# Attention inputs of three batches: 32x32 block transposes on VectorE in place of TensorE transposes

## The chip, the cores and the metric

The kernel runs on one core of one Trainium2 chip. The metric is the device time of one execution in microseconds (us). Before the change three runs took 700.96, 701.54 and 702.19 us, a median of 701.54 us.

The engines are named as in the profile: PE is TensorE's matrix multiply and PEld its weight load, DVE is VectorE, ACT is ScalarE, POOL is GpSimd, SP is SyncE, which issues nearly all loads. Each engine works through its own instructions in order. Where an instruction needs something from another engine or from a transfer, it waits for a semaphore, and all that stands behind it on its engine waits too.

## The reference, cut to what matters

```python
# batch, n_heads, seq_l, seq_g, head_dim = (4, 8, 512, 32, 64)
s_g = scale * np.matmul(q_g, k_all.transpose(0, 1, 3, 2))        # 32 global queries see all 544 keys
out_g = np.matmul(sm(s_g), v_all)
s_ll = scale * np.matmul(q_l, k_l.transpose(0, 1, 3, 2))         # local queries
s_ll = np.where(np.abs(pos[:, None] - pos[None, :]) <= 32, s_ll, -1e9)
s_lg = scale * np.matmul(q_l, k_g.transpose(0, 1, 3, 2))
out_l = np.matmul(sm(np.concatenate([s_lg, s_ll], axis=-1)), np.concatenate([v_g, v_l], axis=2))
x = attn.transpose(0, 2, 1, 3).reshape(2176, 512)
x = relu(x @ w_in) ** 2 @ w_out                                  # 512 -> 2048 -> 512
# then 8 routed experts (512 -> 1024 -> 512), one per token, added to x
```

All inputs and the output are float32. For the scores, queries and keys must lie with the head dimension on the partitions, so the loaded rows have to be turned.

## The kernel before, in words

Attention runs in blocks of 256 local queries: two blocks to a batch, eight in all (j = 0 to 7), each of two tiles "a" and "b" of 128 queries; the batch's 32 global queries ("g") go with them. The dense layer follows one block behind: while `ffn_block(j)` multiplies block j, the attention of block j + 1 is put between its steps. The whole order is written out by hand, as strings of words. `SEQ` holds batch 0 and the first half of batch 1 beside the dense layer's first two blocks and the splitting of its weights; then `EVEN` and `ODD` alternate for dense blocks 2 to 7; then a tail and the experts follow. The order of the words is the order of the instructions on every engine, the queue of SP included. The words that matter here:

- `Lq2`, `Lk10`, `Lk11` in SEQ and `lq`, `lk0`, `lk1` in EVEN and ODD load a query block (`load_q`, L316) or four heads of a batch's keys (`load_k`, L296) into a staging tile of 128 partitions x 1024 floats.
- `2q`, `q` turn a query block (`prep_q`, L357) into `qT`; `20` to `23`, `0` to `3` turn one pair of heads of the keys (`prep_k`, L344) into `kT`, which has place for one batch. In both, PE transposes 128x128 pieces into PSUM (L348 for keys, L365 for queries) and ACT copies them to SBUF (L350, L355, L367). `G` (`prep_globals`) turns the global keys and queries.
- `E` and `F` are steps of the dense layer. Steps come in pairs for a group f of 128 hidden features: `first(f)` is 12 matmuls (L739 to L741) into one of two PSUM places "h"; then ACT takes the ReLU (L743), the square is made on DVE (an `F` or `I` step, L780) or on ACT (`E`, `H`, L782), ACT casts the high part `gh` (L197), POOL or DVE subtracts the low part `gl` (L198), and `second` multiplies (L764 to L766). The square goes out with the step after `first(f)`; `first(f+2)` needs the PSUM place, and so that square. `second` runs one group behind in SEQ, two in EVEN and ODD.
- `V` loads windows of the values (L376, L413), `A` and `C`, `D` assemble and split weights of the dense layer, `r`, `s`, `R00` route, `1b` ends a tile of attention: PE turns it (L294), ACT and DVE split it into `xh` and `xl` (L197, L198), on which the first matmuls of the next dense block work.

The words around the change:

```
SEQ   ... 1g Lq2 C Lk10 A H0 1g I0 2q A C C F0 2G Lk11 E0 I0 20 C E0 21 22 F0 1b F1 23 C D F0 H1 C C V R00 2a ...
EVEN  q E F F r E r a ... E E V g b F b F b F g F s lk1 F g E V g lq F lk0 E
ODD   q E F lq G E 3 2 F 1 E F r E r 0 E r F a r lv0 ...
```

ODD belongs to dense blocks 3 and 5, with the attention blocks 4 and 6 that open batches 2 and 3; there `q` uses what `lq` of the EVEN before loaded. EVEN's `q` serves blocks 3, 5 and 7, whose loads (`Lq3`, and `lq` of ODD) stand most of a dense block ahead. Blocks 0 and 1 (batch 0) are loaded and turned in another way, which the change leaves as it is.

Of the kernel before, what the change touches and what calls it, by code (L numbers as in the profile page):

```python
# [54 lines left out]
def attention_ffn_routed_experts(  # L55
# [22 lines left out]
    nc = tc.nc  # L78
    B, H, SL, D = q_l.shape
    SG = q_g.shape[2]  # L80
    P = 128
# [3 lines left out]
    E, _, F = w1.shape  # L85
    NPAIR = H // 2
# [3 lines left out]
    TPB = SL // P  # L90
    NLT = B * TPB
    NT = NLT + 1
    SEG = 32
    WIN = 3 * SEG
# [7 lines left out]
    BLK = 2 * P  # L102
# [12 lines left out]
    def sb(tag, bufs, shape, name, dtype=F32):  # L115
        return spool.tile(shape, dtype, tag=tag, bufs=bufs, name=name + arm[0])

    def stage(name):
        return wpool.tile([P, 1024], F32, tag="w", name=f"st_{name}{arm[0]}")
# [3 lines left out]
    def pair(name):  # L123
        return ps.tile([P, 4, P], F32, tag="tr", bufs=2, name=name + arm[0])
# [6 lines left out]
    KEYS = (BLOCKS + (BLOCKS - 1) // 3) * SEG  # L131
# [38 lines left out]
    for b in range(B):  # L170
# [11 lines left out]
        out=tri, in_=tri, compare_op=ALU.is_gt, fill=0.0, base=0, pattern=[[1, P]], channel_multiplier=-1,  # L182
# [102 lines left out]
    kT, kin, qT, qin, qgT, vgr = {}, {}, {}, {}, {}, {}  # L285
# [6 lines left out]
    def transposes(o, src, n=P):  # L292
        for p in range(NPAIR):
            nc.tensor.transpose(o[:, p, 0:n], src[0:n, p * P:(p + 1) * P], ident[0:n, 0:n])  # L294

    def load_k(b, z):  # L296

        kin[b, z] = stage(f"k{b}_{z}").rearrange("p (j h d) -> p j h d", h=4, j=TPB)
        if b == 0:
            t = stage(f"k{b}_{z}_in").rearrange("p (h j d) -> p h j d", h=4, j=TPB)
            nc.sync.dma_start(t, k_l[b, 4 * z:4 * z + 4].rearrange("h (p j) d -> p h j d", j=TPB))
            puts[f"{b}{z}"] = lambda: nc.scalar.copy(kin[b, z], t.rearrange("p h j d -> p j h d"))
            return
        for h in range(4):
            nc.sync.dma_start(kin[b, z][:, :, h, :], k_l[b, 4 * z + h].rearrange("(p j) d -> p j d", j=TPB))

    def load_globals(b):  # L310
        t = stage(f"g{b}")
# [4 lines left out]
    def load_q(j):  # L316

        b, z = divmod(j, TPB // 2)
        qin[j] = stage(f"q{j}").rearrange("p (i h d) -> p i h d", h=H, i=2)
        if j < 2:  # L320
            t = stage(f"q{j}_in").rearrange("p (h i d) -> p h i d", h=H, i=2)
            nc.sync.dma_start(t, q_l[b, :, z * BLK:(z + 1) * BLK, :].rearrange("h (p i) d -> p h i d", i=2))
            engine = nc.vector if j == 0 else nc.gpsimd
            puts[str(j)] = lambda: engine.tensor_copy(qin[j], t.rearrange("p h i d -> p i h d"))
            return
        for i in range(2):
            rows = q_l[b, :, z * BLK:(z + 1) * BLK, :].rearrange("h (p i) d -> p i h d", i=2)
            nc.sync.dma_start(qin[j][:, i], rows[:, i])

    def prep_globals(b):  # L330
        kT[b] = sb("kT", 1, [P, NPAIR, KEYS], f"kT{b}")
# [10 lines left out]
        nc.scalar.copy(qgT[b], tr[:, :, 0:SG])  # L342

    def prep_k(b, p):  # L344
        tr = pair(f"ktr{b}_{p}")
        for j in range(TPB):
            two = kin[b, p // 2][:, j, 2 * (p % 2):2 * (p % 2) + 2, :]
            nc.tensor.transpose(tr[:, j, :], two.rearrange("p r d -> p (r d)"), ident)  # L348
        q = WIN * (KEYS // P) // TPB
        nc.scalar.copy(  # L350
            kT[b][:, p, 0:KEYS - SEG].rearrange("p (g q j) -> p j g q", j=TPB, q=P // TPB)[:, :, :, 0:WIN // TPB],
            tr[:, :, 0:q].rearrange("p j (g q) -> p j g q", q=WIN // TPB),
        )
        put = nc.vector.tensor_copy if b == 0 else nc.scalar.copy
        put(kT[b][:, p, KEYS - SEG:KEYS].rearrange("p (q j) -> p j q", j=TPB), tr[:, :, q:P])  # L355

    def prep_q(j):  # L357
        qT[j] = sb("qT", 1, [P, NPAIR, BLK], f"qT{j}")
        for z in range(2):
            tr = pair(f"qtr{j}_{z}").rearrange("p (a i) q -> p a i q", a=2)  # L360
            for a in range(2):
                for i in range(2):
                    h = 2 * (2 * z + a)
                    two = qin[j][:, i, h:h + 2, :]
                    nc.tensor.transpose(tr[:, a, i, :], two.rearrange("p r d -> p (r d)"), ident)  # L365
            for a in range(2):
                nc.scalar.copy(qT[j][:, 2 * z + a, :].rearrange("p (q i) -> p i q", i=2), tr[:, a])  # L367
# [208 lines left out]
    def attention_block(j, S_TAG="s", O_TAG="o", G_TAGS=("s", "o")):  # L576

        b, z = divmod(j, TPB // 2)
        gens = {
            "a": attention(2 * j, S_TAG, O_TAG), "b": attention(2 * j + 1, S_TAG, O_TAG),  # L580
            "g": attention_global(b, *G_TAGS),
        }

        def emit(what):
            if what in gens:
                next(gens[what])
            elif what == "G":
                prep_globals(b)
            elif what == "q":
                prep_q(j)  # L590
            elif what in "0123":
                prep_k(b, int(what))
            elif what == "lq":
                if j + 1 < NB:
                    load_q(j + 1)
            elif what in ("lv0", "lv1"):
                load_v_global(b, int(what[2]))
            elif b + 1 < B:
                load_globals(b + 1) if what == "lg" else load_k(b + 1, int(what[2]))

        return emit
# [649 lines left out]
    with tc.manual_schedule():  # L1251
# [3 lines left out]
        def do(what):  # L1255
# [12 lines left out]
            elif what == "V":  # L1268
                load_v(*divmod(viewed[0], 2))
                viewed[0] += 1  # L1270
            elif what[0] == "P":
                puts[what[1:]]()
            elif what == "L9":
                nc.sync.dma_start(w9[:, :, 0:E], w_gate.rearrange("(k p) e -> p k e", p=P))
                nc.sync.dma_start(w9[:, :, E:E + 1], w_skip.rearrange("(k p o) -> p k o", p=P, o=1))
            elif what[0] == "L":
                load = {"g": load_globals, "k": load_k, "q": load_q, "v": load_v_global}[what[1]]
                load(*map(int, what[2:]))
            elif what[0] in "FEIH":
                square_on[0] = nc.vector if what[0] in "FI" else nc.scalar  # L1280
                rest_on[0] = nc.gpsimd if what[0] in "FE" else nc.vector
                j = int(what[1])
                if j not in streams:
                    streams[j] = ffn_block(j, 1, (("x2", "x2"), ("s", "o"))[j])
                next(streams[j])
            elif what[0] == "R":
                j, z = int(what[1]), int(what[2])
                if (j, z) not in routes:
                    routes[j, z] = route(*outs[j][z], *(("x2",) if j == 0 else ()))
                next(routes[j, z])  # L1290
            else:
                j = int(what[0])
                if j not in emits:
                    emits[j] = attention_block(
                        j, *(("x2", "x2") if j == 2 else ("s", "o")), (("tr", "tr") if j == 1 else ("s", "o"))
                    )
                emits[j](what[1:])
# [15 lines left out]
        for j in range(2, NB):  # L1313
# [4 lines left out]
            for what in (ODD if j % 2 else EVEN).split():  # L1318
# [14 lines left out]
                elif what in route_gens:  # L1333
                    next(route_gens[what])
                    routed += 1
                    if j == NB - 1 and routed == 10:
# [4 lines left out]
                            out=count[:, 0:1], in0=count[:, 0:1], scalar1=2.0 * P, scalar2=None, op0=ALU.max  # L1341
# [29 lines left out]
        for what in TAIL.split():  # L1371
            if what == "T":
                next(ffn, None)
            elif what in "XY":
                j = "XY".index(what)
# [15 lines left out]
            elif what == "S":  # L1391
# [4 lines left out]
                    out=key, in0=key, scalar=float(SEG - P), in1=count[:, FEW[0]:FEW[0] + 1], op0=ALU.add, op1=ALU.max  # L1396
                )
                nc.vector.scalar_tensor_tensor(
                    out=key, in0=count[:, E - 1:E], scalar=float(-P), in1=key, op0=ALU.add, op1=ALU.max
                )  # L1400
                nc.vector.scalar_tensor_tensor(
                    out=key, in0=count[:, 0:1], scalar=float(SEG - 3 * P), in1=key, op0=ALU.add, op1=ALU.max
# [12 lines left out]
            elif what[0] in "gp":  # L1415
                e, j = map(int, what[1:])
# [141 lines left out]
        with tc.If(n_tok[E] <= SEG, label="few") as few:  # L1558
# [12 lines left out]
            n = AFTER * NPE  # L1571
# [71 lines left out]
```

## Time and profile before

| | before |
|---|---|
| runs | 700.96, 701.54, 702.19 us |
| the profiled execution's own time | 701.17 us |
| its span in the profile | 699.5 us |
| PE busy | 675.6 us (97%) in 6661 matmuls |
| DVE busy | 395.9 us (57%) |
| ACT busy | 365.9 us (52%) |
| POOL busy | 165.8 us (24%) |
| DMA queue of the hardware's dynamic transfers | 107296 packets, 70.62 MB |

A timeline row gives the start in us from the span's start, the length, the engine, the line, the operation, what is written from what, and how many are merged; in brackets stands idle time of the engine just before, and what ended it. An instruction row for SP is the issue of a transfer, not the transfer itself. Matmuls overlap: the length of one says less than the distance to the next start.

### The profile page before, as it was taken

The page shows a single profiled execution, that of the slowest core. Times are in us where ns is not written, and L with a number is a line of the kernel's source. Part 1 is how long each engine was busy: PE and PEld are TensorE (multiplying, and loading weights), DVE is VectorE, ACT ScalarE, POOL GpSimd, SP SyncE. Part 2 cuts the span into 40 slices and gives each one's busy share as a digit, 9 for nine tenths or more (in the row PEclk, how much of TensorE's full clock was granted, in tenths as well). Part 3 has the DMA queues.
Part 4 walks back from the last instruction along what each step waited for, and adds up shares of the span by engine and source line. Part 5 has one row for each costly group of instructions (what it writes and reads, how often), then busy time and mean ns, then how long its engine had stood idle before and what let it go on. Part 6 is the DMA issues. An engine that isn't in the chain of part 4 may idle for free. (4 is left out here: it accounts for less than half of the span.)

```text
span 699.5 us, 16771 instructions
## 1 busy us (share of the span) xinstructions
PE 675.6 (97%) x6661; PEld 565.1 (81%) x6661; DVE 395.9 (57%) x1078; ACT 365.9 (52%) x950; POOL 165.8 (24%) x220
## 2 busy tenths in 40 slices
PE   6689998999999999999999999999999999999996
PEld 4466667889888988888898888888887887898876
DVE  1899964872655175265426536534338733915985
ACT  5767568665535655453465445444334414614863
POOL 8000053453212212211212221122220432301311
PEclk9799999999999999999999999999999999999999
DMA  9999644065053501306440210410036688962930
GB/s 271 250 298 281 236 109 90 1 156 103 1 132 84 135 32 36 84 2 143 107 100 32 58 55 9 156 62 1 30 112 186 212 269 301 373 244 85 354 131 21
DMA packets 117695, 93.40 MB, mean 134 GB/s; under 512 B 83733, under 2 KB 90901, under 8 KB 117604
## 3 DMA queue, kind: packets, MB, share of 16 engines
q1 hardware_dynamic: 107296, 70.62, 36.2%
q10 hardware_dynamic: 8292, 15.48, 6.9%
q0 software_dynamic: 2016, 6.09, 2.5%
q8 instruction: 56, 0.92, 0.6%
q14 instruction: 35, 0.29, 0.1%
HBM read 79.91 MB, written 12.66 MB: 132 GB/s over the span
## 5 line engine op out<-in xcount | busy, mean ns | idle before, releaser
L198 POOL TENSOR_TENSOR gl<-g,gh 128x256 fp32r<-128x256 f32 x107 | 79.8, 746 | 297.5 <-ACT gh L197 125.6
L739 PE MATMUL h<-xh,w_in 128*128 128x256 f32 x464 | 134.9, 291 | 0.7 <-ACT xh L197 0.7
L740 PE MATMUL h<-xl,w_in 128*128 128x256 f32 x464 | 129.7, 279 | 0.3 <-DVE xl L198 0.3
L741 PE MATMUL h<-xh,w_in 128*128 128x256 f32 x464 | 129.8, 280 | 0.0
L764 PE MATMUL acc<-w_out,gh 128*128 128x512 f32 x232 | 97.6, 421 | 1.2 <-ACT gh L197 1.2
L766 PE MATMUL acc<-w_out,gl 128*128 128x512 f32 x232 | 91.9, 396 | 0.2
L765 PE MATMUL acc<-w_out,gh 128*128 128x512 f32 x232 | 91.6, 395 | 0.0
L739 PEld LDWEIGHTS h<-xh,w_in 128*128 128x128 f32 x464 | 87.1, 188 | 5.0 <-ACT xh L197 0.9
L740 PEld LDWEIGHTS h<-xl,w_in 128*128 128x128 f32 x464 | 87.2, 188 | 2.6 <-DVE xl L198 0.5
L743 ACT ACTIVATE g<-h 128x256 f32<-128x256 f32 x128 | 48.7, 381 | 74.2 <-PE h L741 44.5
L741 PEld LDWEIGHTS h<-xh,w_in 128*128 128x128 f32 x464 | 87.1, 188 | 0.0
L780 DVE TENSOR_TENSOR g<-h,g 128x256 f32<-128x256 f32 x53 | 22.2, 420 | 85.5 <-ACT g L743 85.4
L464 ACT ACTIVATE sm<-sm,mx 128x128 f32<-128x128 f32 x120 | 46.7, 391 | 44.0 <-DVE mx L462 43.9
L197 ACT CAST gh<-g 128x256 fp32r<-128x256 f32 x116 | 47.2, 407 | 42.8 <-DVE g L780 40.4
L766 PEld LDWEIGHTS acc<-w_out,gl 128*128 128x128 f32 x232 | 43.5, 188 | 12.0 <-POOL gl L198 1.4
L764 PEld LDWEIGHTS acc<-w_out,gh 128*128 128x128 f32 x232 | 43.6, 188 | 8.4 <-ACT gh L197 1.7
L765 PEld LDWEIGHTS acc<-w_out,gh 128*128 128x128 f32 x232 | 43.8, 189 | 5.7
L269 POOL TENSOR_TENSOR w_in<-st_raw_in,w_in 128x512 fp32r<-128x512 f32 x10 | 13.0, 1311 | 76.7 <-ACT w_in L265 76.7
L457 DVE TENSOR_TENSOR sm<-sc,masks_slots 128x512 f32<-128x512 f32 x30 | 20.6, 685 | 15.4 <-PE sc L444 14.4
L782 ACT ACTIVATE g<-g 128x256 f32<-128x256 f32 x63 | 26.3, 417 | 5.0 <-ACT g L743 4.0
L762 PE MATMUL acc<-st_raw_out,gh 128*128 128x512 f32 x48 | 23.9, 618 | 0.8 <-ACT gh L782 0.8
L473 PE MATMUL ptr<-ident,sm 128*128 128x128 f32 x120 | 20.3, 286 | 2.6 <-ACT sm L464 2.4
(638 smaller groups left out, 1463.9 us busy)
## 6 DMA issues: line engine op xcount, KB each, us to landing
st_e<-in_moe_w_dram SPq DMA_DIRECT2D x46, 512.0 KB, 6.5
st_raw_in<-in_moe_w_in_dram SPq DMA_DIRECT2D x16, 512.0 KB, 8.1
st_raw_out<-in_moe_w_out_dram SPq DMA_DIRECT2D x16, 512.0 KB, 8.3
st_e<-in_moe_w_dram ACTq DMA_DIRECT2D x12, 512.0 KB, 7.4
x2d<-x ACTq DMA_DIRECT2D x19, 256.5 KB, 3.6
vr<-in_v_l_dram SPq DMA_DIRECT2D x32, 128.0 KB, 3.3
st_gv<-in_v_l_dram SPq DMA_DIRECT2D x8, 512.0 KB
out_dram<-x ACTq DMA_DIRECT2D x16, 256.0 KB, 3.6
```

The source lines that it names most:

```text
L197: nc.scalar.copy(hi, src)
L198: (lo_engine or nc.vector).tensor_tensor(out=lo, in0=src, in1=hi.bitcast(F32), op=ALU.subtract)
L464: nc.scalar.activation(sm[:, hh, :], sm[:, hh, :], AF.Exp, bias=mx[:, hh:hh + 1], scale=SCALE, accum_out=osum[:, 2 * hh + g:2 * hh + g + 1],)
L739: nc.tensor.matmul(h, lhsT=wh, rhs=xh[:, k, :], start=(k == 0), stop=False)
L740: nc.tensor.matmul(h, lhsT=wh, rhs=xl[:, k, :], start=False, stop=False)
L741: nc.tensor.matmul(h, lhsT=wl, rhs=xh[:, k, :], start=False, stop=(k == KD - 1))
L743: nc.scalar.activation(g, h, AF.Relu)
L762: nc.tensor.matmul(acc[z], lhsT=gh[:, c], rhs=w, start=first_one, stop=last_one)
L764: nc.tensor.matmul(acc[z], lhsT=gh[:, c], rhs=wh, start=first_one, stop=False)
L765: nc.tensor.matmul(acc[z], lhsT=gh[:, c], rhs=wl, start=False, stop=False)
L766: nc.tensor.matmul(acc[z], lhsT=gl[:, c], rhs=wh, start=False, stop=last_one)
L782: nc.scalar.activation(square, g, AF.Square)
```

## The change

For batches 1 to 3 (b > 0, j >= 2) the loads split each head dimension into halves of 32: partition quadrant 2r + half holds head r of a pair and half the head dimension, with positions in blocks of 32 on the quadrant's partitions. A key load of four heads becomes 8 transfers of 64 KB where it was 4 of 128 KB; a query block becomes 16 of 32 KB where it was 2 of 256 KB; the contiguous run falls from 256 to 128 bytes. One 32x32 transpose on each block then puts the head dimension on the partitions. `prep_k` is two DVE transposes to a pair of heads (384 and 128 columns), `prep_q` two of 512 columns; the PE transposes, their PSUM tiles and the ACT copies of these batches are gone. The strings of words are the same.

```diff
+    def quadrants(o, src):
+        for r in range(2):
+            for half in range(2):
+                c = SEG * (2 * r + half)
+                for a in range(o.shape[1]):
+                    nc.sync.dma_start(o[c:c + SEG, a], src(r)[:, a, :, SEG * half:SEG * (half + 1)])
+
     def load_k(b, z):
-        kin[b, z] = stage(f"k{b}_{z}").rearrange("p (j h d) -> p j h d", h=4, j=TPB)
...
-        for h in range(4):
-            nc.sync.dma_start(kin[b, z][:, :, h, :], k_l[b, 4 * z + h].rearrange("(p j) d -> p j d", j=TPB))
+        kin[b, z] = stage(f"k{b}_{z}").rearrange("p (a n d) -> p a n d", a=2, d=SEG)
+        pairs = k_l[b, 4 * z:4 * z + 4].rearrange("(a r) (n p) d -> r p a n d", r=2, p=SEG)
+        quadrants(kin[b, z], lambda r: pairs[r])
...
-        for i in range(2):
-            rows = q_l[b, :, z * BLK:(z + 1) * BLK, :].rearrange("h (p i) d -> p i h d", i=2)
-            nc.sync.dma_start(qin[j][:, i], rows[:, i])
+        qin[j] = stage(f"q{j}").rearrange("p (a n d) -> p a n d", a=NPAIR, d=SEG)
+        pairs = src.rearrange("(a r) (n p) d -> r p a n d", r=2, p=SEG)
+        quadrants(qin[j], lambda r: pairs[r])
...
     def prep_k(b, p):
+        if b:
+            full = WIN * (KEYS // P)
+            src = kin[b, p // 2][:, p % 2].rearrange("p n d -> p (n d)")
+            threes = kT[b][:, p, 0:KEYS - SEG].rearrange("p (g c) -> p g c", c=P)[:, :, 0:WIN]
+            nc.vector.transpose(out=threes, in_=src[:, 0:full].rearrange("p (g c) -> p g c", c=WIN))
+            nc.vector.transpose(out=kT[b][:, p, KEYS - SEG:KEYS], in_=src[:, full:SL])
+            return
...
     def prep_q(j):
         qT[j] = sb("qT", 1, [P, NPAIR, BLK], f"qT{j}")
+        if j >= 2:
+            for a in range(0, NPAIR, 2):
+                nc.vector.transpose(
+                    out=qT[j][:, a:a + 2].rearrange("p a q -> p (a q)"),
+                    in_=qin[j][:, a:a + 2].rearrange("p a n d -> p (a n d)"),
+                )
+            return
```

## Rows read from the trace of the kernel before

**Rows 1.** The page's part 1: busy time by engine

```profile
PE 675.6 (97%) x6661; PEld 565.1 (81%) x6661; DVE 395.9 (57%) x1078; ACT 365.9 (52%) x950; POOL 165.8 (24%) x220
```

**Rows 2.** Stretches: us, busy of PE, PEld, DVE, ACT, POOL; PEclk, DMA share, GB/s

```profile
44.00:690.00 646.00, 640.84 (x6220) 540.21 (x6220) 366.36 (x1016) 338.98 (x878) 150.69 (x158) 1.00 0.43 126
...
98.40:105.50 7.10, 7.10 (x52) 6.04 (x51) 3.02 (x7) 4.91 (x13) 3.28 (x3) 1.00 0.59 134
```

**Rows 3.** PE's transposes by line: min/median/max ns, first and last start

```profile
L348 PE MATMUL ktr<-ident,st_k x64: 270/272/477, 9.0 to 365.0; 128*128 128x128 f32 x64
...
L365 PE MATMUL qtr<-ident,st_q x64: 270/273/474, 12.3 to 410.3; 128*128 128x128 f32 x64
```

**Rows 4.** Timeline of PE, start of dense block 5

```profile
351.41 1.03 PE L365 MATMUL qtr<-ident,st_q 128*128 128x128 f32 x8
352.21 0.36 PE L739 MATMUL h<-xh,w_in 128*128 128x256 f32 x1
...
355.82 0.39 PE L739 MATMUL h<-xh,w_in 128*128 128x256 f32 x1
...
357.34 1.04 PE L348 MATMUL ktr<-ident,st_k 128*128 128x128 f32 x8
358.13 0.48 PE L764 MATMUL acc<-w_out,gh 128*128 128x512 f32 x1
358.45 0.39 PE L765 MATMUL acc<-w_out,gh 128*128 128x512 f32 x1
358.68 0.39 PE L766 MATMUL acc<-w_out,gl 128*128 128x512 f32 x1
```

**Rows 5.** ACT's copies of turned keys and queries, by line

```profile
L350 ACT COPY kT<-ktr x16: 1017/1030/1104, 10.1 to 365.4; 128x480 f32<-128x480 f32 x16
...
L367 ACT COPY qT<-qtr x32: 384/404/430, 13.4 to 411.1; 128x256 f32<-128x256 f32 x32
```

**Rows 6.** Timeline of SP's queue: issues of transfers

```profile
92.45 1.23 SPq L328 DMA_DIRECT2D st_q<-in_q_l_dram  x2
...
110.83 0.45 SPq L413 DMA_DIRECT2D vr<-in_v_g_dram  x1
...
111.32 0.45 SPq L376 DMA_DIRECT2D vr<-in_v_l_dram  x1
...
329.75 1.30 SPq L308 DMA_DIRECT2D st_k<-in_k_l_dram  x2
...
343.35 1.08 SPq L328 DMA_DIRECT2D st_q<-in_q_l_dram  x2
```

**Rows 7.** DMA issues by kind: KB each, median us from issue to landing

```profile
st_k<-in_k_l_dram SPq DMA_DIRECT2D x24, 128.0 KB, 3.3
...
vr<-in_v_l_dram SPq DMA_DIRECT2D x32, 64.0 KB, 2.7
```

**Rows 8.** Timeline of DVE in SEQ, and one copy of 1024 columns by line

```profile
100.18 0.42 DVE L780 TENSOR_TENSOR g<-h,g 128x256 f32<-128x256 f32 x1
...
109.87 0.69 DVE L198 TENSOR_TENSOR xl<-xtr,xh 128x512 fp32r<-128x512 f32 x1 [2.43 <-ACT xh L197]
...
L324 DVE COPY st_q<-st_q_in x1: 693/693/693, 9.6 to 9.6; 128x1024 f32<-128x1024 f32 x1
```

**Rows 9.** Timeline of PE in SEQ, where batch 1 is turned

```profile
103.11 0.40 PE L764 MATMUL acc<-w_out,gh 128*128 128x512 f32 x1
...
110.61 0.38 PE L740 MATMUL h<-xl,w_in 128*128 128x256 f32 x1 [0.34 <-DVE xl L198]
...
112.02 0.60 PE L348 MATMUL ktr<-ident,st_k 128*128 128x128 f32 x4
112.37 0.48 PE L764 MATMUL acc<-w_out,gh 128*128 128x512 f32 x1
```

**Rows 10.** An idle stretch of PE early in the span, and the stretch behind it

```profile
19.90 1.25 PE L473 MATMUL ptr<-ident,sm 128*128 128x128 f32 x3 [2.39 <-ACT sm L464]
...
20.60:23.90 3.30, 3.24 (x70) 2.33 (x69) 3.23 (x7) 2.46 (x12) 0.00 (x0) 0.50 0.85 217
```

More of the change, by code (lines that the diff above doesn't have):

```diff
@@ L294, in transposes @@
             nc.tensor.transpose(o[:, p, 0:n], src[0:n, p * P:(p + 1) * P], ident[0:n, 0:n])
+    def quadrants(o, src):
[4 more added lines that the diff above has]
+                    nc.sync.dma_start(o[c:c + SEG, a], src(r)[:, a, :, SEG * half:SEG * (half + 1)])
     def load_k(b, z):
-        kin[b, z] = stage(f"k{b}_{z}").rearrange("p (j h d) -> p j h d", h=4, j=TPB)
         if b == 0:
+            kin[b, z] = stage(f"k{b}_{z}").rearrange("p (j h d) -> p j h d", h=4, j=TPB)
             t = stage(f"k{b}_{z}_in").rearrange("p (h j d) -> p h j d", h=4, j=TPB)
@@ L318, in load_q @@
         b, z = divmod(j, TPB // 2)
-        qin[j] = stage(f"q{j}").rearrange("p (i h d) -> p i h d", h=H, i=2)
+        src = q_l[b, :, z * BLK:(z + 1) * BLK, :]
         if j < 2:
+            qin[j] = stage(f"q{j}").rearrange("p (i h d) -> p i h d", h=H, i=2)
             t = stage(f"q{j}_in").rearrange("p (h i d) -> p h i d", h=H, i=2)
-            nc.sync.dma_start(t, q_l[b, :, z * BLK:(z + 1) * BLK, :].rearrange("h (p i) d -> p h i d", i=2))
+            nc.sync.dma_start(t, src.rearrange("h (p i) d -> p h i d", i=2))
             engine = nc.vector if j == 0 else nc.gpsimd
```

## The prediction, made before the change was run

> **What bounds the kernel now.** I read the busy times first: PE works 97% of the span, the others 57% or less [rows 1]. The table of stretches says where that holds: from 44 to 690 us PE is busy for 640.84 of 646.00 us at full granted clock [rows 2]. All turning of batches 1 to 3 lies in there. So what leaves PE is time won, as long as PE finds its next operands ready; and any wait that the change puts in front of PE is time lost.
>
> Two queues decide whether operands are ready. DVE now has to wait for the loads in its own order, and behind that wait stand the squares of the dense layer and, in SEQ, the low part `xl` (L198), without which PE has no work. SP issues the loads one by one. The timeline of SP's queue, read beside that of PE, is therefore the second view that matters.
>
> **What goes from PE.** 64 transposes each for keys and queries [rows 3]; a quarter is batch 0's and stays, so 48 + 48 go. Each is listed at 270 ns or more, but they overlap, so I take distances between starts. Eight for a query block: 351.41 to 352.21, 0.80 us. Eight for two pairs of heads: 357.34 to 358.13, 0.79 [rows 4]. Four: 112.02 to 112.37, 0.35 [rows 9]. The matmul behind such a group also starts its successor late, 0.32 us (358.13 to 358.45) against 0.23 (358.45 to 358.68) [rows 4], 0.09 to a group. A query block is 0.89 us, a batch of keys 0.79 + 2 x 0.35 + 3 x 0.09 = 1.76. For six query blocks and three batches that makes 10.6 us, 1.5% of the time. This is the most that can be won.
>
> Here a rule and the rows disagree. The Trainium skill, "VectorE: DVE Perf Modes", section "The three transpose paths", gives 390 ns for a 128x128 bf16 transpose on TensorE; an estimate by that page is 96 x 0.39 = 37 us removed. The rows are of float32 in a full pipeline and show 0.10 us each, and I go by them.
>
> **What ACT loses.** 24 copies of about 1.03 us, 24 of 0.40 [rows 5] and the short ones. I cost it at nothing: ACT is half idle and PE does not wait for it.
>
> **What DVE gains.** No row shows a block transpose. Operations of 512 and 256 columns take 0.69 and 0.42 us; a copy of 1024 columns takes 0.693 [rows 8]. The bounds for 512 columns are thus 0.35 (the copy's rate) and 1.38 (two passes); I take 0.69, the nearest in columns, and by the same line 0.55 for 384 and 0.28 for 128. A query block is 1.38 us, a pair of heads 0.83; together 18 us on an engine that is 57% busy. Away from the waits below, one step is covered by the group that `second` lags behind, so it costs nothing by itself.
>
> **What SP gains.** A query block grows from 2 transfers to 16, a tile of keys from 4 to 8. Transfers of 64 KB with 256 runs follow each other after 0.49 us (110.83 to 111.32); the new query transfers also have 256 runs each, of half the length. Two key transfers of 512 runs take 1.30 us, so 0.67 each with the gap; the new ones also have 512. A query block took 1.08 or 1.23 us and will take 16 x 0.49 = 7.8; a tile of keys goes from 2.7 to 5.4 us [rows 6]. The bounds for a query transfer are 0.25 (half, if the issue goes by bytes) and 0.67. Landing comes 2.7 us after issue for 64 KB and 3.3 for keys [rows 7]. The engines behind the queue have room: in a stretch with only runs of 256 bytes they moved 134 GB/s at 0.59 busy [rows 2], so a run costs at most 18 ns on an engine, and a query block of 4096 runs 4.6 us on 16 of them, less than its issue.
>
> The Trainium skill speaks against this: "DMA: Bandwidth & Descriptors", section "Rules for kernel authors", wants small transfers put together and calls those under 64 KB mostly overhead. With its fixed 2.0 us paid one after another (an estimate), a query block would take 32 us and the change would lose tens of us; the rows show issues 0.49 apart, each landing in its own 2.7, so I price by issues.
>
> **Where it falls on the path.** Three places.
>
> EVEN, blocks 3, 5, 7: the queries are loaded most of a block ahead, so DVE finds them landed. Gain 0.89 x 3 = 2.67.
>
> ODD, blocks 4 and 6, shown for 6. `lq` is issued from 343.35 [rows 6]; the sixteenth transfer goes at 343.35 + 15 x 0.49 = 350.7 and lands at 353.4. Two transposes: 354.8; the square behind them: 355.2. The third `first` needs that square's PSUM place. It started at 355.82 [rows 4], without PE's query transposes it could at 354.93, so PE loses 0.3. `lk0`, behind `lq`, lands at 351.2 + 7 x 0.67 + 3.3 = 359.2; DVE holds there, but the next square's place is wanted only later. Gain 0.89 + 1.76 - 0.3 = 2.35, twice: 4.7. Later loads on SP slip some 9 us (6.7 + 2.7 of added issue), in front of long waits of SP for window places.
>
> SEQ: three loads in a row. `Lq2` is issued from 92.45 [rows 6], lands at 92.45 + 7.35 + 2.7 = 102.5, is turned by 103.9, and the square that ran at 100.18 [rows 8] follows some 5 us late. PE stands from about 102 to 107.7, where `second` began at 103.11 [rows 9]. The 16 key transfers follow from 100.3; the last goes at 110.3 and lands at 113.6. Behind it on DVE stand pair 2 (0.83), a square (0.42) and `xl` (0.69): 115.6. PE's first matmul on `xl` stood at 110.61 [rows 9], having waited for it already. From there to `second` at 112.37 it was 1.76, now 1.32 without four transposes: 116.9. So SEQ as a whole loses 4.5 us, its own savings counted.
>
> PE's clock may add to that: early in the span an idle stretch of 2.39 us was followed by one at granted clock 0.50, the lower level of 1.2 GHz, for all of 3.3 us [rows 10]. Here the first idle stretch would be followed by work that waits for `xl` anyway: 4.6 us of it between 107.7 and 115.6, which even with 3.3 us at half speed is done. I count 0, with 2 as the upper end.
>
> **Sum.** 4.5 - 4.7 - 2.67 = -2.9 us on the profiled execution's 701.17, 698.3; its span is 1.7 shorter than that. The median of the runs stands 0.37 higher, so I forecast 698.7. With clock and issue prices near the rows the forecast's own range is 696 to 702.
>
> **Rivals.**
>
> *The loads stay hidden.* If query transfers issue at 0.25 us, `lq` lands at 349.8 and SEQ's keys about 4 us earlier; with landings as short as the queue's room allows, little is left of the waits. Then the whole 10.6 goes: 690.9. For it: the engines' room, and no wait of PE for these loads now. Against it: no issue on SP's queue in the rows is that short.
>
> *SP's queue puts the loads behind their use, and it is slower than before.* At 0.67 us for a query transfer, `lq` lands at 343.35 + 10.05 + 2.7 = 356.1, its square ends at 357.9, PE stands 3.0 us: ODD loses 0.35, twice. SEQ's last key lands at 116.5, `second` begins at 119.8 instead of 112.37: 7.4. Sum 0.7 + 7.4 - 2.67 = +5.4, 706.9; if the two idle stretches in ODD bring the low clock for 3.3 us each, another 3.3: 710. It decides from about 0.55 us an issue, as each 0.1 costs 1.6 in SEQ and 1.5 in each ODD. For it: transfers with 512 runs take 0.67, and the source now has one more step. Against: the run count is the same as in the 0.49 rows.
>
> *Transposes at twice the price* (1.38 for 512 columns): each ODD loses 1.38 more, SEQ 0.83: +3.6, 702.3. For it: nothing but that no row shows one.
>
> **Chances.** A difference under 0.2%, 1.4 us, can't be told from no change. Forecast 0.48 (0.36 of it faster, 0.12 the same), hidden 0.12 (faster), slow queue 0.27 (slower), dear transposes 0.13 (0.08 the same, 0.05 slower). That is 0.48 faster, 0.20 the same, 0.32 slower. The range goes from 692.5, just above the hidden case, to 707, which takes in the slow queue without clock loss.
>
> **What would show it.** Right: SP issues of queries 0.49 apart; DVE idle before the transposes of query block 2 until about 102.5 and of keys until about 113.6; PE idle in SEQ ahead of the `second` after `2G` and of the first matmul on `xl`, and almost none in ODD; then PE 10 us less busy. Wrong: query issues over 0.55 or under 0.4 apart; transposes of 512 columns far from 0.69; PE idle of some us at the start of ODD; a clock under 1.00 after 100 us.

## The result, and the profile after

| | before | after |
|---|---|---|
| median of the runs | 701.72 us (700.96 to 702.19, 4 runs) | 708.26 us (706.82 to 710.51, 4 runs) |
| the profiled execution's own time, its span | 701.17, 699.5 us | 710.51, 708.8 us |
| mean granted clock over the span | 0.99 | 0.98 |

The kernel is slower: the ratio of the times is 1.0097, with a 95% interval of 1.0068 to 1.0126. The forecast was 698.7 us, in a range up to 707.0. The profiled execution is the slowest of the four after, so some 3 of the 9.3 us between the two spans are not in the medians.

The page of the kernel after, busy time and two groups of part 5 (busy us, mean ns, then idle time before them and what ended it), answers [rows 1]:

```profile
PE 670.8 (95%) x6565; PEld 559.2 (79%) x6565; DVE 411.9 (58%) x1114; ACT 347.5 (49%) x902; POOL 165.8 (23%) x220
...
L758 PE MATMUL h<-xh,w_in 128*128 128x256 f32 x464 | 136.0, 293 | 7.7 <-DVE g L799 5.1
...
L783 PE MATMUL acc<-w_out,gh 128*128 128x512 f32 x232 | 98.7, 426 | 3.9 <-ACT gh L197 3.9
```

The same two groups on the page of the kernel before:

```profile
L739 PE MATMUL h<-xh,w_in 128*128 128x256 f32 x464 | 134.9, 291 | 0.7 <-ACT xh L197 0.7
...
L764 PE MATMUL acc<-w_out,gh 128*128 128x512 f32 x232 | 97.6, 421 | 1.2 <-ACT gh L197 1.2
```

The 96 transposes are gone from PE (6661 matmuls became 6565), yet PE is only 4.8 us less busy, and in front of the first matmuls of `first` it now sits idle 7.7 us where it was 0.7; 5.1 of them end with the square on DVE. The table of stretches says why the busy time hardly fell. Its columns are those of [rows 2]:

```profile
44.00:690.00 646.00, 629.89 (x6023) 529.24 (x6022) 374.12 (x1040) 314.58 (x820) 149.18 (x157) 0.99 0.44 125
...
104.30:107.70 3.40, 3.40 (x10) 2.63 (x11) 1.99 (x5) 1.89 (x5) 1.93 (x2) 0.51 0.78 126
114.60:118.00 3.40, 3.40 (x14) 3.01 (x14) 0.63 (x3) 1.50 (x4) 0.27 (x1) 0.50 0.73 165
240.90:244.30 3.40, 3.40 (x14) 3.30 (x15) 1.27 (x4) 2.51 (x7) 1.47 (x2) 0.50 0.66 106
360.30:367.10 6.80, 5.19 (x18) 4.71 (x19) 3.78 (x10) 2.94 (x8) 2.20 (x3) 0.50 0.63 103
```

Four stretches that had full clock before run at 0.50, the lower level of 1.2 GHz. Each begins at the end of an idle stretch of PE, within 1.6 us before or after it. The timeline of PE shows these four (in brackets the idle time, and what ended it):

```profile
104.22 0.71 PE L783 MATMUL acc<-w_out,gh 128*128 128x512 f32 x1 [2.73 <-ACT gh L197]
...
113.35 0.39 PE L758 MATMUL h<-xh,w_in 128*128 128x256 f32 x1 [2.65 <-ACT xh L197]
...
240.89 0.58 PE L758 MATMUL h<-xh,w_in 128*128 128x256 f32 x1 [2.01 <-DVE g L799]
...
361.91 0.58 PE L758 MATMUL h<-xh,w_in 128*128 128x256 f32 x1 [3.09 <-DVE g L799]
```

The first two are in SEQ, where [rows 9] had a wait of 0.34. The other two stand at the third `first` of dense blocks 3 and 5 (ODD), which in [rows 4] started without a wait, at 355.82. The timeline of DVE in block 5 shows what came late there:

```profile
359.80 0.71 DVE L373 STREAM_TRANSPOSE qT<-st_q 128x512 f32<-128x512 f32 x1 [6.72 <-DMA st_q<-in_q_l_dram]
360.69 0.71 DVE L373 STREAM_TRANSPOSE qT<-st_q 128x512 f32<-128x512 f32 x1 [0.18 <-DMA st_q<-in_q_l_dram]
361.43 0.42 DVE L799 TENSOR_TENSOR g<-h,g 128x256 f32<-128x256 f32 x1
```

DVE stands 6.72 us for the query load, two transposes follow, then the square, and PE starts at once: the chain that the prediction drew, some 6 us later than drawn. Of these, 2.5 are there before the load begins: it is issued from 345.88, where the prediction had 343.35. The rest is on SP's queue (issue, length of the group of issues), against [rows 6]:

```profile
91.65 7.76 SPq L301 DMA_DIRECT2D st_q<-in_q_l_dram  x16
99.51 8.74 SPq L301 DMA_DIRECT2D st_k<-in_k_l_dram  x16
...
226.99 11.07 SPq L301 DMA_DIRECT2D st_q<-in_q_l_dram  x16
...
345.88 13.38 SPq L301 DMA_DIRECT2D st_q<-in_q_l_dram  x16
```

The same 16 transfers take 7.76 us in SEQ, 0.485 each, but 11.07 and 13.38 in the two EVENs that load for ODD. Narrower windows show the hole: two transfers from 226.99, nothing for 3.2 us, then the other fourteen. The first row is the answer for 226.9 to 228.1, the second that for 231.1 to 239:

```profile
226.99 0.95 SPq L301 DMA_DIRECT2D st_q<-in_q_l_dram  x2
...
231.15 6.91 SPq L301 DMA_DIRECT2D st_q<-in_q_l_dram  x14
```

The waits of SP's queue between 345 and 360 us name what it waits for in the second of them, in front of the third and fourth transfer (us in total, times, longest):

```profile
SPq L301 <- DMA x2d<-x: 4.3, 1, 4.3
SPq L301 <- DMA out_dram<-x: 1.5, 1, 1.5
```

A load of queries waits for stores of the routing. These two stores are issued on ACT's queue (timeline of ACT, both EVENs):

```profile
228.36 0.33 ACTq L639 DMA_DIRECT2D x2d<-x  x1
228.72 0.45 ACTq L640 DMA_DIRECT2D out_dram<-x  x1
...
348.30 0.33 ACTq L639 DMA_DIRECT2D x2d<-x  x1
```

There is no data between them and the queries. The semaphore events of the trace give the reason: the transfers of SP and ACT report their completion on eight semaphores, taken in turn in the order of the program, and each waits until the transfer before it on its semaphore has landed.

| transfer | issued | semaphore | landed |
|---|---|---|---|
| queries, first and second | 226.99, 227.49 | 108, 109 | 228.91, 229.38 |
| ACT's store x2d | 228.36 | 110 | 231.13 |
| ACT's store out_dram | 228.72 | 101 | 231.64 |
| queries, third | 231.15 | 110 | 232.91 |
| queries, fourth | 231.66 | 101 | 233.43 |

The third query transfer goes 0.02 us after the store on 110 has landed. A load of two transfers needed two of the eight places; one of sixteen goes through all of them twice, and meets whatever slow transfer sits on one. The stores stand earlier in the program but are issued by ACT behind its own work, 1.4 us after SP's first query transfer.

The start of the same PE instruction in both profiled executions, after minus before, gives the bill by stretch (in us, to about 0.2, by where a boundary is drawn):

| stretch | forecast | measured |
|---|---|---|
| opening | 0 | -0.9 |
| SEQ | +4.5 | +5.4 |
| EVEN, blocks 3, 5, 7 | -0.9 each | -1.0, -0.7, -0.7 |
| ODD, block 4 | -2.35 | +1.1 |
| ODD, block 6 | -2.35 | +2.9 |
| the experts' start, at 603.5 us | 0 | +1.7 |
| the rest | 0 | +1.5 |

One step is of another kind. At 603.48 PE stood 1.58 us with nothing that the profile shows to release it. The rest, +1.5, lies behind 680 us; there every other trace of this case, that of the control included, also stands 0.4 to 2.0 us above this one trace of before, so it can't be put down to the change, nor can the -0.9 of the opening, where the other traces stand at -1.4 to +1.4. The stop in the timeline of PE:

```profile
603.48 0.50 PE L1101 MATMUL eh_a<-e0l,xp 128*128 128x512 f32 x1 [1.58 <-issue]
```

### The profile page after: what moved, and what is told of

It reads as the page before. It is cut to its first block, busy times and chain, and to the rows that moved or that the text cites. A ratio compares the mean times of both kernels' runs of the same rounds, so it can differ in the third digit from the quotient of the medians.

```text
span 708.8 us, 16711 instructions
## 1 busy us (share of the span) xinstructions
PE 670.8 (95%) x6565; PEld 559.2 (79%) x6565; DVE 411.9 (58%) x1114; ACT 347.5 (49%) x902; POOL 165.8 (23%) x220
## 5 line engine op out<-in xcount | busy, mean ns | idle before, releaser
L758 PE MATMUL h<-xh,w_in 128*128 128x256 f32 x464 | 136.0, 293 | 7.7 <-DVE g L799 5.1
L759 PE MATMUL h<-xl,w_in 128*128 128x256 f32 x464 | 131.4, 283 | 0.3 <-DVE xl L198 0.3
L760 PE MATMUL h<-xh,w_in 128*128 128x256 f32 x464 | 131.4, 283 | 0.0
L783 PE MATMUL acc<-w_out,gh 128*128 128x512 f32 x232 | 98.7, 426 | 3.9 <-ACT gh L197 3.9
L758 PEld LDWEIGHTS h<-xh,w_in 128*128 128x128 f32 x464 | 88.9, 191 | 12.7 <-DVE g L799 5.3
L784 PE MATMUL acc<-w_out,gh 128*128 128x512 f32 x232 | 92.9, 400 | 0.0
L759 PEld LDWEIGHTS h<-xl,w_in 128*128 128x128 f32 x464 | 88.9, 192 | 3.3 <-DVE xl L198 0.7
L760 PEld LDWEIGHTS h<-xh,w_in 128*128 128x128 f32 x464 | 88.7, 191 | 0.0
L783 PEld LDWEIGHTS acc<-w_out,gh 128*128 128x128 f32 x232 | 44.5, 192 | 11.3 <-ACT gh L197 4.5
L784 PEld LDWEIGHTS acc<-w_out,gh 128*128 128x128 f32 x232 | 44.7, 193 | 5.8
```

The lines of the kernel that those rows point to most:

```text
L758: nc.tensor.matmul(h, lhsT=wh, rhs=xh[:, k, :], start=(k == 0), stop=False)
L759: nc.tensor.matmul(h, lhsT=wh, rhs=xl[:, k, :], start=False, stop=False)
L760: nc.tensor.matmul(h, lhsT=wl, rhs=xh[:, k, :], start=False, stop=(k == KD - 1))
L783: nc.tensor.matmul(acc[z], lhsT=gh[:, c], rhs=wh, start=first_one, stop=False)
L784: nc.tensor.matmul(acc[z], lhsT=gh[:, c], rhs=wl, start=False, stop=False)
```

## Experiments

The theory after the result: ODD loses because query transfers wait for places that ACT's stores hold; SEQ loses because three loads in a row put DVE late, as predicted; and each idle stretch of PE costs the clock on top. Rivals: the loads are simply too long for the lead they have, whatever the stores do; or DVE's added work, or the keys, are what costs. Each kernel was traced in one execution only, and executions of one kernel differ by up to 7.5 us; where the traced one lies far from the median, its time is given. Code cuts are shortened, against the kernel after unless it says otherwise.

**Keys alone.** Loads and turning of keys as after, queries as before (`load_q` and `prep_q` unchanged):

```diff
-        if j >= 2:
-            for a in range(0, NPAIR, 2):
-                nc.vector.transpose(out=qT[j]..., in_=qin[j]...)
-            return
```

> Keys of batches 1 to 3 as in the change, local queries as before it. Theory (T1): the loss sits in the sixteen-transfer query load, whose transfers each wait for a completion semaphore that only eight transfers of SP's and ACT's queues share in turn, so that the load in front of ODD waits for ACT's stores; DVE holds the square behind it, PE idles and its clock falls. Without the query load the key part wins: 1.76 us in each of ODD, about 0 to 1 in SEQ, so 697 to 699 us and no idle stretch of PE at the start of ODD. Rival (T2): DVE's transposes and the doubled key transfers cost as much themselves: 703 to 706.

Measured 701.76 us, ratio 0.9998 (0.9988 to 1.0008): no change, between the two expectations. Each ODD gains 1.6 us by the starts of its matmuls, close to the 1.76 that a batch of keys was priced at, and PE has no idle stretch there. SEQ loses 2.8 even so (98 to 118 us, where the change loses 5.2): DVE holds at the third pair of heads, `xl` follows behind it, PE stands 2.87 us, and the clock is at 0.50 for 6.8 us behind that. PE's row:

```profile
111.48 0.58 PE L750 MATMUL h<-xh,w_in 128*128 128x256 f32 x1 [2.87 <-ACT xh L197]
```

**Queries alone.** The reverse:

```diff
-        if b:
-            full = WIN * (KEYS // P)
...
-            return
```

> Local queries as in the change, keys as before it. T1: the whole loss stays here: PE idle of 2 to 3 us at the start of both ODD blocks and of some 2.7 us in SEQ, low clock behind them, 705 to 709 us. T2: half of the loss, 703 to 705.

Measured 705.52 us, ratio 1.005 (1.0034 to 1.0066), at the lower edge of what was expected. The traced execution took 702.79. In it SEQ loses 4.2 us (98 to 118 us; idle 2.96 ahead of `second`, then low clock). In ODD the expected 2 to 3 us of idle PE did not come. The hole is shorter, since with four key transfers instead of eight the turn of the semaphores comes out differently and the sixth transfer meets the store: SP's waits between 344 and 362 us are

```profile
SPq L301 <- DMA x2d<-x: 1.9, 1, 1.9
SPq L301 <- DMA out_dram<-x: 0.4, 1, 0.4
```

and PE stands only 0.42 us at the third `first`, without a loss of clock. So sixteen transfers need not cost ODD its loss. How the slower executions of this kernel spent their 3 us more, no trace shows.

**The store earlier.** The change, with EVEN's last `s`, which issues the two stores, two steps earlier:

```diff
-    b F b F g F s lk1 F g E V g lq F lk0 E
+    b F s b F g F lk1 F g E V g lq F lk0 E
```

> The change, with EVEN's last routing step (it ends in ACT's two stores of 256 KB) put two dense steps earlier; the loads stay where they are. T1: the sixteen query transfers in front of ODD issue 0.49 us apart without the holes of 3.1 to 4.3 and 1.5 us that end when the stores land; they land by 236 and 356; PE idle at ODD's start falls under 1 us and the clock stays up there: 6 to 8 us less than the change, 700 to 703. Rival (T2: it is the number of transfers on SP, the stores only happen at that time): within 1.5 us of the change, 707 to 709.

Measured 700.81 us, ratio to before 0.9982 (0.9964 to 0.9999): 7.4 us better than the change by the medians, from the place of one word. In block 5 the sixteen transfers follow each other without a hole:

```profile
347.00 8.78 SPq L301 DMA_DIRECT2D st_q<-in_q_l_dram  x16
```

The wait for the store is shorter, but not gone. It has moved to the window load in front of the query load, in block 3 and in block 5 (waits of SP, 225 to 245 and 344 to 362 us):

```profile
SPq L432 <- DMA x2d<-x: 3.2, 1, 3.2
...
SPq L432 <- DMA x2d<-x: 2.2, 1, 2.2
```

So the last query transfer leaves only 1.0 us earlier than in the change in block 3, and 3.5 in block 5. PE still stands 1.24 and 0.66 us in the two ODDs, where less than 1 was expected and the prediction had 0.3, and behind the 1.24 the clock is at 0.50 for 3.4 us. By the starts ODD comes to +0.2 and -1.9 us, where the change had +1.1 and +2.9. That the loads alone are too long falls in the main: with the same loads two thirds of what ODD missed are gone. The traced execution was the slowest, 706.82; its extra time is a stop of 2.79 us at the experts' start, of the kind shown above, with 3.4 us of low clock behind it, 4.6 us together.

**SEQ in another order.** The turning of query block 2 moved behind `I0`, that of the keys spread over later steps:

```diff
-    ... H0 1g I0 2q A C C F0 2G Lk11 E0 I0 20 C E0 21
-    22 F0 1b F1 23 C D F0 H1 C C V R00 2a F1 ...
+    ... H0 1g I0 A C C F0 2G Lk11 E0 I0 2q C E0
+    F0 1b F1 20 21 C D F0 H1 22 C C V R00 23 2a F1 ...
```

> The change, with the turning words of SEQ alone put later (2q behind I0, 20 and 21 behind F1, 22 behind H1, 23 in front of 2a); all loads stay. If the loss of about 5 us up to 118 us is DVE waiting in order in front of the square and xl, PE's two idle stretches of 2.7 us there go, the clock stays up, and 5 to 7 us are won: 701 to 703. Rival (T3: the later landing itself delays the scores of 2a, whatever DVE's order): under 2 us, 706 to 708.

Measured 703.01 us, ratio 1.0001 (0.998 to 1.0021), at the upper end of the first expectation. SEQ gains 1.5 us by the starts (from -0.8 to -2.3) where the change loses 5.2, and the clock stays at 1.00 there; the 0.67 us in front of `xh` are those of the kernel before. ODD is as bad as ever:

```profile
106.91 0.39 PE L758 MATMUL h<-xh,w_in 128*128 128x256 f32 x1 [0.67 <-ACT xh L197]
...
234.06 0.39 PE L758 MATMUL h<-xh,w_in 128*128 128x256 f32 x1 [1.80 <-DVE g L799]
```

SEQ's loss is thus the order in which DVE meets the waits. With the same loads and the same transposes PE keeps 1.5 of the 2.65 us that leave it there; 0.59 go into a wait of PE for keys that are turned late.

**The query load earlier.** Instead of the store, `lq` two steps forward:

```diff
-    b F b F g F s lk1 F g E V g lq F lk0 E
+    b F b F g F s lk1 lq F g E V g F lk0 E
```

> The change, with lq put in front of the last V and g of EVEN (behind lk1), so that the sixteen query transfers go out before SP waits for window places and before ACT's stores. T1: they land 8 us or more before ODD needs them, PE does not stand at ODD's start and both ODD blocks win about 2.35 us instead of losing 1.1 and 2.9: 8 to 9 us less than the change, 698 to 701 with SEQ's loss of 5 us left. T2 (DVE's transposes themselves hold the squares in ODD): PE still idles a microsecond or more there, 703 to 706.

Measured 706.12 us, ratio 1.005 (1.0031 to 1.0069). Both expectations were too low. The traced execution took 703.92. In it the idle stretch at ODD's start is gone, but SP now reaches the eighth query transfer 9 us before the store on its semaphore is issued at all and waits 11.8 us, and all that stands behind it on SP waits as well. SP, DVE and PE in block 5:

```profile
331.45 20.48 SPq L301 DMA_DIRECT2D st_q<-in_q_l_dram  x16
...
355.29 4.26 SPq L301 DMA_DIRECT2D st_k<-in_k_l_dram  x8
```

```profile
362.86 0.68 DVE L354 STREAM_TRANSPOSE kT<-st_k 128x480 f32<-128x480 f32 x1 [5.30 <-DMA st_k<-in_k_l_dram]
```

```profile
364.92 0.19 PE L680 MATMUL pl<-w,x2T 128*128 128x27 bf16 x1 [1.12 <-ACT x2T L668]
366.38 0.19 PE L680 MATMUL pl<-w,x2T 128*128 128x27 bf16 x1 [1.27 <-DVE x2T L659]
367.10 0.41 PE L680 MATMUL pl<-w,x2T 128*128 128x27 bf16 x10 [0.54 <-DVE x2T L660]
```

The load takes 20.48 us instead of 13.38, `lk0` goes out at 355.29, and DVE, holding for these keys, is late for the thirds (three bf16 parts) of the routing's operand. An early load that waits for a semaphore is a late load for its successors.

**SEQ and query load both.** The two edits together:

> The change with lq in front of the last V and g of EVEN and SEQ's turning words later. If the transposes leave PE for DVE at no cost once the loads land ahead of their use, nearly the whole 10.6 us come out: PE idle under 1 us at each place, full granted clock from 40 us to the end, 691 to 694 us. If moving work to DVE has a cost of its own, 696 or more.

Measured 699.96 us, ratio 0.9973 (0.9959 to 0.9988): better than before, but in the range of the second expectation. The trace (of an execution of 698.52 us) shows what is left, and it is not the transposes' own price. PE's clock is at 1.00 from 34 to 692 us. The routing's idle stretches stay (1.23 and 0.54 us in block 3; 0.60, 1.27 and 0.54 in block 5), and PE's stop without a releaser is there again, 1.28 us. In ODD the keys, behind the held query load, leave late here too.

**48 small matmuls in the opening, added to the change.**

```diff
+            for _ in range(48):
+                nc.tensor.matmul(o[0:32, 0:16], lhsT=idle[:, 0:32], rhs=idle[:, 0:16], start=True, stop=True)
```

> The change, with 48 matmuls of 16 columns more at the very start, where PE has nothing to do for 2.3 us. They only move the place of PE's later instructions in its stream. If PE's idle stretch of 1.0 to 2.8 us at about 602 us in the change and its variants, which ends at no semaphore, is PE waiting for its own instructions to be loaded, it goes (keys_only and queries_only, with as many fewer matmuls, do not show it): 1.5 to 3 us less than the change. If it comes from the experts' weights or their conversion, it stays, and the time is within 1 us of the change.

Measured 709.15 us, ratio 1.0094 (1.0079 to 1.0109): no gain. The stop near 600 us is gone, but one of the same kind has come at an earlier place (waits of PE: us, times, longest),

```profile
PE po L501 <- issue: 2.1, 1, 2.1
```

and the idle stretches of SEQ and ODD came out longer in this execution (3.65, 3.38 and 2.89 us).

**The same 48 with both moves.**

> Both moves together with the 48 small matmuls at the start. If the instruction place costs 1 to 3 us, 689 to 692 us; if not, the same as both moves within 1 us.

Measured 696.88 us, ratio 0.992 (0.9907 to 0.9933), in a spread of 1.6 us: 3.1 us less than without the 48, and in neither expected range. No stop without a releaser of 1 us or more is left. In the two traces that stop is worth 1.5 us; the other half isn't explained.

**The control: the same 48 in the kernel before.**

> The kernel before with 48 small matmuls of 32x16 more in the opening, as a control for the runs that have them. If they only move the place at which PE has to wait for its own instructions, the kernel before, which shows no such wait behind 44 us, gains nothing: 701.0 to 702.5 us, or 703 to 705 if the 48 bring such a wait into it. If they help in another way (the opening, the clock), it gains what the kernel with both moves gained by them, about 3 us: 698 to 699.

Measured 702.51 us, ratio 1.0004 (0.9992 to 1.0017): alone they bring nothing. Here a stop without a releaser appears at the attention's matmuls (1.8 us in two; the traced execution took 704.28). So the 48 can bring such a stop as well as take one away.

**SEQ in the other order, the store earlier, and the 48.** `lq` and `lk0` stay in their place, `s` stands as in the experiment with the store:

> SEQ's query load later and in pieces, the last store of a routing two steps earlier in EVEN, lq and lk0 in their old place, 48 small matmuls in the opening. If ODD's loss is only the wait of SP's query transfers for the completion of ACT's stores: 700.8 with the store early, less about 5 for SEQ, less 0 to 2 for the instruction wait, 694 to 697, with PE idle at ODD's start of 1.3 us or less. If lq must also be issued earlier than this, PE idles 2 us or more at each ODD start and the time is 698 or more.

Measured 696.79 us, ratio 0.9938 (0.9915 to 0.996). The time is where it was expected, but the runs spread from 694.2 to 701.7; PE's idle stretch at block 3's start is 1.69 us, a little above the bound, though with no loss of clock.

**All three moves and the 48.**

```diff
-    b F b F g F s lk1 F g E V g lq F lk0 E
+    b F s b F g F lk1 lq F g E V g F lk0 E
```

> SEQ later, lq two steps earlier and the store two steps earlier as well, 48 small matmuls. If the 1.2 and 1.7 us of idle PE ahead of the routing's matmuls in the kernel with both moves came from lk0, which stood behind 16 query transfers that waited for the stores, they go and lq costs nothing: 693 to 695.5. If they come because DVE turns keys ahead of the routing's thirds wherever lk0 lands, they stay: 696 to 698.

Measured 693.98 us (692.54 to 695.08), ratio 0.9883 (0.9864 to 0.9902): the best of all, 8.2 us under the kernel before by the ratio. The clock is full from 34 to 689 us, and the keys of block 5 leave at 347.98, where with both moves and the 48 they left at 352.21; PE's work is 2.0 us earlier here as a whole, so the keys have gained 2.2 us on it:

```profile
34.00:689.00 655.00, 643.41 (x6313) 540.41 (x6301) 394.27 (x1075) 326.88 (x848) 154.57 (x159) 1.00 0.45 129
```

```profile
325.54 19.09 SPq L301 DMA_DIRECT2D st_q<-in_q_l_dram  x16
...
347.98 4.79 SPq L301 DMA_DIRECT2D st_k<-in_k_l_dram  x8
```

The query load still has its hole (19.09 us), but early enough that PE does not wait for it. The two longer waits of the routing are gone, as the first expectation says: they came from keys that landed late.

**The three moves without the 48.**

> SEQ later, lq and the store two steps earlier, without the 48 small matmuls. If the three moves carry the gain and PE's wait for its own instructions near 590 us returns without the 48: 1 to 3 us more than with them, 695 to 697, with an idle stretch of PE of 1 us or more that nothing in the profile releases. If the 48 do nothing: 693.5 to 694.5 and no such stretch.

Measured 694.78 us (694.61 to 695.24), ratio 0.9906 (0.9889 to 0.9922). PE's stop is back, 1.53 us, as expected, and no other idle stretch over 0.8 us came back with it. The medians differ by 0.8 us, the ratios by 1.6 us, and their intervals overlap, so what the 48 give in time isn't settled; the three moves carry most of the gain, some 6.6 of 8.2 us by the ratios.

## Why the prediction was wrong

**The step that failed** is ODD: "the sixteenth transfer goes at 343.35 + 15 x 0.49 = 350.7 and lands at 353.4". The issue price was right, 0.485 to 0.49 wherever nothing holds the queue, and the landing even shorter than priced, 1.9 us in the median instead of 2.7. What failed is the assumption that issues follow each other unhindered. The third and fourth transfer waited 4.3 and 1.5 us for the semaphores of ACT's stores; in block 6 DVE's second transpose began at 360.69 where the forecast had both done at 354.8 (2.5 us of that the load's later start), and PE stood 3.09 us instead of 0.3. Against the forecast the two ODDs missed by 3.45 and 5.25 us. That is 8.7 of the 12.2 us by which this execution missed its 698.3, and 2.9 of the 8.7 are low clock behind the two stops; the median missed by 9.6. The store's place shows the cause: with `s` two steps earlier the hole in the load and two thirds of the miss went.

**The clock**: "I count 0, with 2 as the upper end." The starts slip by 1.1 us more through each stretch of 3.4 us at 0.50, and by 1.8 through the one of 6.8, about 5 in all, of which some 4 stay. The first 1.1, in SEQ, are hidden as the prediction argued: PE then waits 2.65 us for `xh` behind keys that DVE gets at 111.30, whatever PE's clock. But that second idle stretch brought the low clock once more, on work that had no wait to hide in, and ODD's stops, which were forecast at 0.3 us, brought it twice.

**SEQ** was right in its mechanism, and near in its size, +5.4 for +4.5, by luck: errors offset each other. The queries landed earlier than priced, so PE's first stop was 2.73 us, up to 104.22, and not from 102 to 107.7. The key transfers issue in 8.74 us instead of 10.7 (0.53 to 0.55 each, not 0.67), so DVE's third pair began at 111.30, where the forecast had the keys landing at 113.6 (0.8 of it because the loads began at 91.65 and not 92.45). Against that, between the square behind this pair and `xl` DVE waits another 0.96 us for ACT, which casts `gh` and `xh`, and the low clock behind the second stop took 1.1; the forecast had neither.

**What leaves PE** was right: with the waits out of the way (all three moves and the 48), the starts gain 8.7 us of the 10.6 from 98 us to the experts, ODD 2.5 and 2.1 to 2.7 (by where its end is drawn) against 0.89 + 1.76 = 2.65, EVEN 0.7 to 0.9 each against 0.89. In SEQ, which keeps 1.5 of 2.65, part of it goes into a wait for the keys that were turned later.

**The transposes** were right in price: the kernel after, DVE by line and form, shows (busy, mean ns, idle before)

```profile
L373 DVE STREAM_TRANSPOSE qT<-st_q 128x512 f32<-128x512 f32 x12 | 8.2, 699 | 15.0 <-DMA st_q<-in_q_l_dram 15.0
L354 DVE STREAM_TRANSPOSE kT<-st_k 128x480 f32<-128x480 f32 x12 | 7.9, 662 | 3.9 <-issue 3.4 <-DMA st_q<-in_q_l_dram 0.5
L355 DVE STREAM_TRANSPOSE kT<-st_k 128x32 f32<-128x32 f32 x12 | 2.0, 169 | 0.0
```

0.70 us for 512 columns against 0.69. A pair of heads splits into 480 and 32 columns, not 384 and 128 as the text ahead of the prediction has it; the sum is 0.83 all the same (0.66 + 0.17). The rival with transposes at twice the price falls. Of the copies that left ACT, [rows 5] give 12 of 1.03 us, not 24: L350 has 16 in all, four to a batch. They were priced at nothing, so the sum stands, but no run separates what they gave.

**The rivals.** The time came out next to the one of the slow queue (706.9, or 710 with the clock), which was given 0.27, but not by its mechanism: it decides from 0.55 us an issue, and the issue stayed below. Its loss in ODD was right in kind, a square behind a late query load. The rule of the Trainium skill, "DMA: Bandwidth & Descriptors", section "Rules for kernel authors", that small transfers are to be put together, points the right way here, though not through its overhead: 32 KB landed 1.9 us after issue in the median, with the next issues overlapping. What sixteen transfers cost more than two, beside 7.8 us of issue, is places in the turn of semaphores.

**Not foreseen:** PE's stop at the experts' start. Its 1.0 to 2.8 us stand in all six traces of the change and its moves without the 48, and in none of the other eight, and nothing in the profile releases it. That PE waits for its own instructions fits this, but no run shows it directly, and it stays open.

**What the trace of before had shown:** SP's queue already waited for the x2d store ahead of key loads (waits of SP):

```profile
SPq L308 <- DMA x2d<-x: 8.6, 4, 3.7
```

The prediction read the issues' lengths and gaps, but not the waits of that queue.

## What to carry to other kernels

When a transfer is cut into many, ask not only what one issue costs but what each issue waits for: read the waits of the issuing queue, and look which slow transfers of other queues share its completion semaphores. A load that gets longer has to move forward together with those it shares places with; moved alone, here, it held up the loads behind it. Look for the low clock behind an idle stretch of PE: behind 40 us, each one of 2.01 us or more in these traces came with it, at a price of 1.1 us for 3.4 us of it, unless a later wait hides that.

## What was not expected of the hardware

- An idle stretch of PE of 1.24 us (the store moved), 1.80 (SEQ reordered), 2.01 or more (the change) was followed by the low clock; one of 1.69 (SEQ and store, with the 48) and those of 0.42 to 0.74 were not. Three in a row of 1.12, 1.27 and 0.54 were (`lq` alone moved), two of 1.23 and 0.54 were not.
- Query transfers of 32 KB in runs of 128 bytes landed 1.9 us after issue in the median of 96 (1.7 to 7.9), against 2.7 for 64 KB in runs of 256 bytes [rows 7].
- Moving one word changed the time by 7.4 us (the change, and the change with the store earlier), against at most 10.6 that the removal of 96 transposes could give.
